# Attention and two mixture-of-experts stages on one core: counts in h's bank, later weight conversions, a shorter expert 3

## The chip, the cores and the metric

The kernel runs on one core of a Trainium2 chip. Its engines are PE (TensorE, with its weight loads shown as PEld), DVE (VectorE), ACT (ScalarE), POOL (GpSimd) and SP (SyncE); each runs its own list of instructions in order and meets the others by semaphores. The metric is the time of one execution on the device in microseconds (us), the median of several runs; lower is better.

## What is computed

Three steps follow one another. Attention over 4 batches of 8 heads has 576 positions, a head size of 64, a window of 128 positions and a bias that falls with distance. Its output, 2304 tokens of 512 numbers, goes through a dense layer, and that layer's result through eight experts of which each token takes one or none:

```python
h = x @ w_in                       # 512 -> 2048
g = s * np.maximum(h, 0.0)**2 + b
x = g @ w_out                      # 2048 -> 512
do_compute = x @ w_skip > 0        # the other tokens are passed on as they are
e_idx, gate_w = argmax and softmax of x @ w_gate over 8 experts
out[token] = x[token] + gate_w * (np.maximum(x[token] @ w1[e], 0) @ w2[e])
```

All of it is fp32. How many tokens each expert gets depends on the data: 639, 194, 63, 83, 51, 20, 167 and 143 for the inputs used here.

## The kernel before

**Products.** Each fp32 product is made of three products of a rounded type: an operand is split into a high part (names that end in h, made on ACT by a cast) and a low part (names that end in l, made on DVE by subtraction, helper `lower`, L77), and high by high, high by low and low by high are added up in PSUM.

**Dense layer.** The tokens are taken in six blocks (j = 0 to 5) of 384, and each block in 16 steps (m = 0 to 15, loop L704 to L752). One step is `g1(j, m)` (L457: 12 matmuls into the PSUM tile `h_ps`, then ACT's relu of it into `r`, L467, and DVE's square `r<-r,sb`, L468), `g1_split` (L471: `gh` on ACT, L477, and `gl` on DVE, L478) and `g2` of the step before (L483: nine matmuls into the three tiles `acc`). So PE runs 12 matmuls of h(m), nine of acc(m-1), 12 of h(m+1), and so on, in an order that the code writes out by hand (a chain from matmul to matmul, helper `mm`, L135). `h_ps` has one bank, "h", and `r` one buffer, so the relu of a step has to wait for `gl` of the step before. The bursts of the attention and its transposes (`t_ps`, in bank "at", copied to `pt` on ACT) and products (`o_ps`) stand between these steps where `events` (L331 to L352) puts them.

**Routing.** After a block, `logits` (DVE, three a step in the last block) and `route` (L532 to L640) work out for each token its expert and its place in that expert's list. In it two small matmuls count the tokens of each expert (L584 and L585, out of `oh` into `p_ps`, in bank "at"), DVE adds these counts to the running ones (`bs`, `v`, `cnt`, L601 to L603), and after more DVE work (`rk`, `di`) POOL writes the tokens' numbers into the lists in DRAM (`lst<-pay,di`, L637). For blocks 0 to 3 the counting stands in the next block but one, behind h of step 1; the counts of block 4 stand in the last block, behind step 10.

**Last block (j = 5).** While it runs, the weights of the first experts arrive in two ring buffers and are split, one piece after each step (`split`, L655: ACT's cast `wh<-ring`, L663, then DVE's `wl`, after which SP loads the next piece). The generator `moe2` is started there too (`later`): when the lists of blocks 0 to 4 are in DRAM, SP reads a part of them (`la<-lst`, L973), POOL gathers expert 0's first tokens by it (`two<-x2d,la`, L796), and PE transposes them (`x_t`, L799: `p_x<-cst,two`, L803) ahead of the last nine matmuls of acc.

**Experts.** `expert(e)` (L959) branches on the number of tiles of 128 tokens: `pair` (L925) for two or more, else `single` (L880). PE fetches its instructions as it goes, and `hint` (L858) tells it ahead of time where the branch of the next expert will lead. `FURTHER` (L33) says how many further pairs of tiles are written out in code for an expert ahead of a loop that takes the rest. `fin` (L841) makes an expert's result (`og`, DVE L843), `h_t` (L849) transposes the hidden layer (`p_t` on PE, `hth` on ACT, `htl` on DVE), and `conv` splits weight pieces for later experts.

## Time and profile before

| | us |
|---|---|
| median of three runs (743.21 to 746.54) | 743.6 |
| the profiled execution | 747.76 |
| its span, first to last instruction | 745.9 |
| PE busy in it | 719.0 (96%) |
| DVE busy | 522.3 (70%) |
| ACT busy | 373.1 (50%) |

The profile is of one execution, which took 4.2 us longer than the median. PE is busy nearly all the time, so what matters is where PE stands still, for whom, and in which stretches it was granted half its clock. Times in the rows are counted from the span's start. The attention and blocks 0 to 5 take up the time to about 545, the routing of the last block and expert 0 the time to about 604, and experts 1 to 7 the rest.

### The profile page before, as it was taken

The numbers are of one execution on the slowest core, as the hardware profiler recorded it, in microseconds if no ns is written. First come the engines' busy times: TensorE is split into PE (matmuls) and PEld (weight loads), VectorE is DVE, ScalarE is ACT, GpSimd is POOL, SyncE is SP. The second block draws the span as 40 slices with busy tenths as digits, with TensorE's granted clock in tenths as the row PEclk, the third lists the DMA queues.
The fourth block names the chain that finished last, engine by engine and source line by source line (L and its number), as shares of the span: only waits on it lengthen the run. The fifth ranks groups of instructions, "written<-read, shape, count | busy, mean of one in ns | idle before, by whom it ended". The sixth has DMA issues, their size and how long they took to land. (4 is left out here: it accounts for less than half of the span.)

```text
span 745.9 us, 13019 instructions
## 1 busy us (share of the span) xinstructions
PE 719.0 (96%) x4532; PEld 616.7 (83%) x4532; DVE 522.3 (70%) x1544; ACT 373.1 (50%) x889; POOL 61.3 (8%) x66
## 2 busy tenths in 40 slices
PE   6789999999999999999999999999999999899995
PEld 4468888888888888788888888988888888787994
DVE  4989999767677676777777665799753245799341
ACT  5766777544564444555555333445441134688230
POOL 0000000000001000100000100010205310312011
PEclk9779999999999999999999999999999999999999
DMA  8986441522324221432123111455442642989000
GB/s 244 294 279 177 132 142 40 168 68 81 93 61 125 54 68 54 138 92 80 54 79 110 31 42 43 156 173 180 128 170 81 226 137 79 359 293 383 19 21 17
DMA packets 50911, 96.40 MB, mean 129 GB/s; under 512 B 8874, under 2 KB 26282, under 8 KB 50816
## 3 DMA queue, kind: packets, MB, share of 16 engines
q1 hardware_dynamic: 45744, 86.35, 36.0%
q0 software_dynamic: 3296, 5.60, 2.3%
q10 hardware_dynamic: 1776, 3.28, 1.2%
q8 instruction: 49, 0.80, 0.4%
q14 instruction: 46, 0.38, 0.2%
HBM read 84.89 MB, written 13.65 MB: 132 GB/s over the span
## 5 line engine op out<-in xcount | busy, mean ns | idle before, releaser
L135 PE MATMUL h_ps<-xh,wh 128*128 128x384 f32 x380 | 132.4, 348 | 0.7 <-ACT r L467 0.7
L135 PE MATMUL h_ps<-xh,wl 128*128 128x384 f32 x380 | 128.9, 339 | 0.0
L135 PE MATMUL h_ps<-xl,wh 128*128 128x384 f32 x380 | 128.8, 339 | 0.0
L467 ACT ACTIVATE r<-h_ps 128x384 f32<-128x384 f32 x96 | 47.1, 490 | 135.5 <-PE h_ps L135 115.3
L468 DVE SCALAR_TENSOR_TENSOR r<-r,sb 128x384 f32<-128x384 f32 x96 | 59.1, 616 | 58.6 <-ACT r L467 57.6
L529 DVE CUSTOM_DVE_ANT_0 junk<-x,hp 128x512 bf16<-128x512 f32 x135 | 92.8, 688 | 1.6
L135 PE MATMUL acc<-wh,gh 128*128 128x512 f32 x288 | 86.4, 408 | 0.0
L177 ACT ACTIVATE tp<-tp,stat 128x256 f32<-128x256 f32 (+2 forms) x160 | 74.8, 469 | 19.4 <-DVE stat L169 19.3
L135 PE MATMUL acc<-wh,gl 128*128 128x512 f32 x288 | 83.0, 396 | 0.0
L135 PE MATMUL acc<-wl,gh 128*128 128x512 f32 x288 | 82.5, 394 | 0.0
L477 ACT ACTIVATE gh<-r,sb 128x384 fp32r<-128x384 f32 x96 | 59.1, 616 | 40.5 <-DVE r L468 40.3
L478 DVE SCALAR_TENSOR_TENSOR gl<-r,sb,gh 128x384 fp32r<-128x384 f32 x96 | 59.0, 615 | 28.2 <-ACT gh L477 28.0
L135 PEld LDWEIGHTS h_ps<-xh,wh 128*128 128x128 f32 x380 | 71.9, 189 | 6.9 <-issue 2.7
L135 PEld LDWEIGHTS h_ps<-xl,wh 128*128 128x128 f32 x380 | 72.0, 189 | 2.6
L135 PEld LDWEIGHTS h_ps<-xh,wl 128*128 128x128 f32 x380 | 71.9, 189 | 0.3 <-DVE wl L77 0.3
L135 PEld LDWEIGHTS acc<-wh,gl 128*128 128x128 f32 x288 | 53.9, 189 | 13.6 <-DVE gl L478 0.9
L135 PEld LDWEIGHTS acc<-wl,gh 128*128 128x128 f32 x288 | 54.1, 188 | 12.5
L169 DVE CUSTOM_DVE_ANT_0 tp<-s_ps,masks 128x256 f32<-128x256 f32 (+2 forms) x160 | 52.7, 377 | 10.5 <-PE t_ps L133 4.5
L637 POOL DMA_INDIRECT lst<-pay,di x18 | 18.5, 1030 | 490.9 <-DVE di L634 486.9
L135 PEld LDWEIGHTS acc<-wh,gh 128*128 128x128 f32 x288 | 50.0, 188 | 7.6 <-issue 3.1
L838 PE MATMUL p_o<-wh,hth 128*128 128x512 f32 x120 | 48.7, 405 | 0.3 <-ACT hth L854 0.2
L838 PE MATMUL p_o<-wl,hth 128*128 128x512 f32 x120 | 47.4, 395 | 0.0
(165 smaller groups left out, 1249.9 us busy)
## 6 DMA issues: line engine op xcount, KB each, us to landing
w_words<-wm SPq DMA_DIRECT2D x30, 512.0 KB
more<-we SPq DMA_DIRECT2D x30, 512.0 KB
ring<-we SPq DMA_DIRECT2D x28, 512.0 KB
hp<-wgt SPq DMA_DIRECT2D x45, 256.0 KB
vt<-vl SPq DMA_DIRECT2D x32, 192.0 KB
x2d<-x SPq DMA_DIRECT2D x17, 256.0 KB
out<-x SPq DMA_DIRECT2D x17, 256.0 KB
q<-q_in SPq DMA_DIRECT2D x16, 192.0 KB
```

Source lines behind the costliest of these rows:

```text
L135: i = f(*args, **kw)
L169: anchor['v'] = nc.vector.tensor_tensor_reduce(out=t[0:nr, i, c0:c0 + n], in0=ps[i][0:nr, c0:c0 + n], in1=masks[0:nr, 2 * units[u][1] + i, ...
L177: anchor['s'] = nc.scalar.activation(out=t[0:nr, i, c0:c0 + n], in_=t[0:nr, i, c0:c0 + n], func=ACTF.Exp, scale=-1.0, bias=st[0:nr, 0, i:i ...
L467: nc.scalar.activation(out=r, in_=hp, func=ACTF.Relu)
L468: nc.vector.scalar_tensor_tensor(out=r, in0=r, scalar=sb[:, 0:1], in1=r, op0=ALU.mult, op1=ALU.mult)
L477: nc.scalar.activation(out=gh, in_=r, func=ACTF.Identity, bias=sb[:, 1:2])
L478: i = nc.vector.scalar_tensor_tensor(out=gl, in0=r, scalar=sb[:, 1:2], in1=gh.bitcast(F32), op0=ALU.add, op1=ALU.subtract)
L529: nc.vector.tensor_tensor_reduce(out=junk, in0=x2t[j, t], in1=w, scale=1.0, scalar=0.0, op0=ALU.mult, op1=ALU.add, accum_out=lgs[j][:, t, ...
L637: i = nc.gpsimd.indirect_dma_start(out=lst, out_offset=bass.IndirectOffsetOnAxis(ap=di[:, t:t + 1], axis=0), in_=pay[:, t, :], in_offset=N ...
L838: last = nc.tensor.matmul(p_o[s], lhsT=h[:, c, s * 128:s * 128 + 128], rhs=w[p, 4 + c // 2][:, o:o + 512], start=cs[0] == 0 and n == 0, st ...
```

## The change

It has six parts. (1) The counts of blocks 0 to 3 go into columns 384 to 431 of the bank that holds `h_ps`, which is now taken whole (128 x 512), in place of bank "at". (2) In the last burst of the attention, the two transposing turns stand at 0.65 and 0.85 of the interval in place of 0.55 and 1. (3) In the last block, `h_ps` takes banks "h" and "as0" in turn, and the weight pieces are split behind `gh` on ACT and behind `gl` on DVE, at steps 1 to 13 and 15, with two more after the block's result; before, one was split at each of the 16 steps. (4) Expert 3 has no further pair written out, and the hint of expert 3's one-tile code stands two matmuls into the second half of its second product. (5) In `single`, the last piece of weights is split behind `fin` and `h_t`. (6) In `pair`, the second tile is transposed into a bank of `p_h`.

```diff
--- before.py
+++ after.py
@@ -30,7 +30,8 @@
 UB = 3
 CONV = (6, 7, 8, 9, 10, 11, 12)
 LAST = NE - 1
-FURTHER = (2, 0, 0, 1, 0, 0, 0, 0)
+LATE = 3
+FURTHER = (2, 0, 0, 0, 0, 0, 0, 0)
 
 
 
@@ -344,7 +345,7 @@
             d, at = first + i, 1 + wait + i * n_seg / n
             ev.append((at, burst, d))
             gs = groups[2 * d:2 * d + 2]
-            ts = [at + n_seg / n * f for f in ((0.55, 1) if j else (0.65, 0.85))]
+            ts = [at + n_seg / n * f for f in ((0.55, 1) if j and d + 1 < (len(groups) + 1) // 2 else (0.65, 0.85))]
             if ceil(ts[0]) == ceil(ts[1]):
                 ev.append((ts[1], turn2, gs))
             else:
@@ -455,8 +456,13 @@
     acc = {}
     UNTIL = [1, 2, 3, 4, 5, 5]
 
+    hs = {}
+
     def g1(j, m):
-        hp = bank("h", [128, TB], "h_ps")
+
+        hp = bank("as0" if j == NB - 1 and m % 2 else "h", [128, 512], "h_ps")
+        hs[j] = hp
+        hp = hp[:, 0:TB]
         n = 0
         for k in range(4):
             for w, x in ((wh[m], xh), (wh[m], xl), (wl[m], xh)):
@@ -474,11 +480,11 @@
         gh = M.tile([128, TB], F32R, name="gh", tag="gh", bufs=2)
         gl = M.tile([128, TB], F32R, name="gl", tag="gl", bufs=2)
 
-        nc.scalar.activation(out=gh, in_=r, func=ACTF.Identity, bias=sb[:, 1:2])
+        a = nc.scalar.activation(out=gh, in_=r, func=ACTF.Identity, bias=sb[:, 1:2])
         i = nc.vector.scalar_tensor_tensor(out=gl, in0=r, scalar=sb[:, 1:2], in1=gh.bitcast(F32),
                                            op0=ALU.add, op1=ALU.subtract)
         gt[j, m] = (gh, gl)
-        return i
+        return a, i
 
     def g2(j, m, ps=(0, 1, 2)):
         gh, gl = gt[j, m]
@@ -573,14 +579,14 @@
         off = rc[:, 8:16].unsqueeze(1).to_broadcast([128, TPB, NE])
         de = small([128, TPB], "de")
         eo = small([128, TPB], "eo", U32)
-        if j < NB - 1:
-            pp = bank("at", [128, 2, TPB, NE], "p_ps")
-        else:
-            pp = bank("as0", [128, 2, TPB, NE], "p_ps")
         f = nc.tensor.matmul
         if j < NB - 2:
             yield
+
+            pp = hs[j + 2][:, TB:TB + 2 * TPB * NE].rearrange("p (a t e) -> p a t e", a=2, t=TPB)
             f = lambda *args, **kw: mm(nc.tensor.matmul, *args, **kw)
+        else:
+            pp = bank("at" if j < NB - 1 else "as0", [128, 2, TPB, NE], "p_ps")
         f(pp[:, 0], lhsT=ustrict, rhs=oh.rearrange("p t e -> p (t e)"), start=True, stop=True)
         last = f(pp[:, 1], lhsT=ones, rhs=oh.rearrange("p t e -> p (t e)"), start=True, stop=True)
         nc.vector.tensor_tensor(out=v, in0=oh, in1=off, op=ALU.mult)
@@ -652,7 +658,7 @@
             eng.dma_start(out=ws.at[ws.loaded], in_=we[PIECES[ws.loaded]])
             ws.loaded += 1
 
-    def split():
+    def split(act=None, dve=None):
         n = ws.split
         t, i = PIECES[n]
         p = t % 2
@@ -660,8 +666,10 @@
             eh[p, i] = W(8 * p + i, "wh")
             el[p, i] = W(8 * p + i, "wl")
         raw = ws.at.pop(n)
-        nc.scalar.copy(eh[p, i], raw)
-        lower(el[p, i], raw, eh[p, i])
+        with tc.issue_after(act) if act else ExitStack():
+            nc.scalar.copy(eh[p, i], raw)
+        with tc.issue_after(dve) if dve else ExitStack():
+            lower(el[p, i], raw, eh[p, i])
         ws.free.append(raw)
         ws.split = n + 1
         pump()
@@ -719,7 +727,7 @@
                 next(counting, None)
                 counting = None
             attn_until(2 * m + 1)
-            done = g1_split(j, m)
+            biased, done = g1_split(j, m)
             if j == 0:
                 w_step()
             if m:
@@ -743,11 +751,16 @@
                     counting = route(j - 1)
                     next(counting, None)
             if j == NB - 1 and m in (10, 15):
-                later(None)
-            if j == NB - 1:
+                order[0] = later(None) or order[0]
+
+            if j == NB - 1 and 0 < m < NM - 2:
+                split(biased.ins, done.ins)
+            if j == NB - 1 and m == NM - 1:
                 split()
     last = g2(NB - 1, NM - 1)
     evac(NB - 1)
+    split()
+    split()
     spare = later(last.ins)
     for _ in route(NB - 1):
         pass
@@ -831,12 +844,14 @@
             nc.scalar.activation(out=h, in_=ps, func=ACTF.Relu)
             nc.vector.scalar_tensor_tensor(out=l, in0=ps, scalar=0.0, in1=h.bitcast(F32), op0=ALU.max, op1=ALU.subtract)
 
-    def gemm2(p, s, f, cs=None):
+    def gemm2(p, s, f, cs=None, then=None):
         cs = cs or range(4 * f, 4 * f + 4)
         for n, (c, h, w) in enumerate([(c, hth, w) for c in cs for w in (eh, el)] + [(c, htl, eh) for c in cs]):
             o = (c % 2) * 512
             last = nc.tensor.matmul(p_o[s], lhsT=h[:, c, s * 128:s * 128 + 128], rhs=w[p, 4 + c // 2][:, o:o + 512],
                                     start=cs[0] == 0 and n == 0, stop=cs[-1] == 7 and n == 3 * len(cs) - 1)
+            if n == 1 and then:
+                hint(*then)
         return last
 
     def fin(s, x, e, k):
@@ -888,16 +903,18 @@
         gemm1(e % 2, 0)
         conv(own)
         gemm1(e % 2, 1)
-        hint(e + 1, 1)
+        if e != LATE:
+            hint(e + 1, 1)
         conv(new, 2)
         gemm2((e - 1) % 2, 1, 0)
         if e < LAST:
             x_t(one[(e + 1) % 4], 0)
-        conv(new)
-        gemm2((e - 1) % 2, 1, 1)
+        conv(new, 1)
+        gemm2((e - 1) % 2, 1, 1, then=(e + 1, 1) if e == LATE else None)
         fin(1, *rest(e - 1))
         h_t()
         nc.vector.tensor_copy(la[:, e, 1, :], la[:, e, 0, :])
+        conv(new)
         if e == LAST:
             second(e)
             fin(1, one[e % 4], e, 1)
@@ -926,7 +943,7 @@
 
         left = rest(e if e == 0 else e - 1)
         own = [p for p in NEED[e] if p[0] == e] if e else []
-        x_t(rows1[0], 1)
+        x_t(rows1[0], 1, p_h[1])
         conv(own, 2)
         second(e - (e > 0))
         fin(1, *left)
@@ -974,9 +991,9 @@
     gather(0, 0, two[1], NT - TB)
     yield
     p_x = bank("at", "p_x")
-    x_t(two[1], 0)
-
-    with tc.issue_after((yield)):
+    last = x_t(two[1], 0)
+
+    with tc.issue_after((yield last.ins)):
         p_h = [bank("ao", "p_h0"), bank("as1", "p_h1")]
         gemm1(0, 0, (0, 1))
     with tc.issue_after((yield og)):
```

What stands where, from the two programs, with the semaphores that an instruction waits for in brackets. PE in block 3, behind h of step 1 (`oh` and `cst` are the operands of the counts), before:

```order
L135 MATMUL h_ps<-xl,wh_354 128x384
L135 MATMUL h_ps<-xh,wl_355 128x384
L135 MATMUL p_ps<-oh,cst 128x24 [waits DVE_49,PE_49]
L135 MATMUL p_ps<-oh,cst 128x24
L135 MATMUL t_ps<-cst,tp 128x128 [waits DVE_49,PE_49]
L135 MATMUL t_ps<-cst,tp 128x128 x3
L135 MATMUL acc<-wh_273,gh 128x512 [waits Activation_49]
```

and now:

```order
L136 MATMUL h_ps<-xl,wh_354 128x384
L136 MATMUL h_ps<-xh,wl_355 128x384
L136 MATMUL h_ps<-oh,cst 128x24 [waits Activation_49]
L136 MATMUL h_ps<-oh,cst 128x24
L136 MATMUL t_ps<-cst,tp 128x128 [waits DVE_49,PE_49]
L136 MATMUL t_ps<-cst,tp 128x128
L136 MATMUL t_ps<-cst,tp 128x128 [waits DVE_49]
L136 MATMUL t_ps<-cst,tp 128x128
L136 MATMUL acc<-wh_273,gh 128x512
L136 MATMUL acc<-wh_273,gh 128x512 [waits DVE_49]
```

The counts waited for DVE and PE, and wait for ACT now; `t_ps`, which waited for DVE's use of the counts, waits for its own operand.

DVE in the last block, behind the square of step 12 and the sums of block 4's counts (the rows named `r<-r,sb` are the squares of step 13 and later; the last two instructions `di<-rk,di` and `di<-di,eo` make the places that POOL's list writing waits for), before:

```order
L629 TENSOR_REDUCE rk<-v 128x3 [waits DVE_49]
L599 COPY bs<-cnt 128x8 [waits DVE_49]
L632 TENSOR_SCALAR di<-rk 128x3 [waits DVE_49]
L633 SCALAR_TENSOR_TENSOR di<-rk,di 128x3 [waits DVE_49]
L634 TENSOR_TENSOR di<-di,eo 128x3 [waits DVE_49]
L77 TENSOR_TENSOR wl_6086<-ring_5484,wh_6085 128x1024 [waits DMAHW4_49,Activation_49]
L478 SCALAR_TENSOR_TENSOR gl<-r,sb,gh 128x384 [waits Activation_49]
L468 SCALAR_TENSOR_TENSOR r<-r,sb 128x384 [waits Activation_49]
L77 TENSOR_TENSOR wl_6120<-ring_5483,wh_6119 128x1024 [waits DMAHW5_49,Activation_49]
L478 SCALAR_TENSOR_TENSOR gl<-r,sb,gh 128x384 [waits Activation_49]
```

and now:

```order
L635 TENSOR_REDUCE rk<-v 128x3 [waits DVE_49]
L605 COPY bs<-cnt 128x8 [waits DVE_49]
L638 TENSOR_SCALAR di<-rk 128x3 [waits DVE_49]
L78 TENSOR_TENSOR wl_6111<-ring_5480,wh_6110 128x1024 [waits DMAHW4_49,Activation_49]
L639 SCALAR_TENSOR_TENSOR di<-rk,di 128x3 [waits DVE_49]
L474 SCALAR_TENSOR_TENSOR r<-r,sb 128x384 [waits Activation_49]
L640 TENSOR_TENSOR di<-di,eo 128x3 [waits DVE_49]
L484 SCALAR_TENSOR_TENSOR gl<-r,sb,gh 128x384 [waits PE_49,Activation_49]
L78 TENSOR_TENSOR wl_6145<-ring_5479,wh_6144 128x1024 [waits DMAHW5_49,Activation_49]
L474 SCALAR_TENSOR_TENSOR r<-r,sb 128x384 [waits Activation_49]
L484 SCALAR_TENSOR_TENSOR gl<-r,sb,gh 128x384 [waits PE_49,Activation_49]
L474 SCALAR_TENSOR_TENSOR r<-r,sb 128x384 [waits Activation_49]
```

The last `di` stood ahead of the conversion `wl` and of the next step's `r`; it stands behind both. `gl` stands ahead of the step's `wl` and no longer behind it.

DVE at the end of expert 5, before:

```order
L806 TENSOR_TENSOR xtl<-p_x,xth 128x4x128 [waits Activation_49]
L77 TENSOR_TENSOR wl_6052<-more_6480,wh_6051 128x1024 [waits DMAHW0_49,Activation_49]
L77 TENSOR_TENSOR wl_6086<-more_6481,wh_6085 128x1024 [waits DMAHW1_49,Activation_49]
L843 SCALAR_TENSOR_TENSOR og<-p_o_6360,la,one_6033 128x512 [waits DMASW3_49,DMASW5_49,DMASW2_49,DMASW6_49,DVE_49,PE_49]
L855 TENSOR_TENSOR htl<-p_t_6358,hth 128x4x128 [waits Activation_49]
L855 TENSOR_TENSOR htl<-p_t_6359,hth 128x4x128 [waits Activation_49]
L900 COPY la<-la 128x2 [waits DMASW0_49]
L964 UNCONDITIONAL_BRANCH
```

and now:

```order
L819 TENSOR_TENSOR xtl<-p_x,xth 128x4x128 [waits Activation_49]
L78 TENSOR_TENSOR wl_6077<-more_6476,wh_6076 128x1024 [waits DMAHW0_49,Activation_49]
L858 SCALAR_TENSOR_TENSOR og<-p_o_6356,la,one_6024 128x512 [waits DMASW3_49,DMASW5_49,DMASW2_49,DMASW6_49,DVE_49,PE_49]
L870 TENSOR_TENSOR htl<-p_t_6354,hth 128x4x128 [waits Activation_49]
L870 TENSOR_TENSOR htl<-p_t_6355,hth 128x4x128 [waits Activation_49]
L916 COPY la<-la 128x2 [waits DMASW0_49]
L78 TENSOR_TENSOR wl_6111<-more_6477,wh_6110 128x1024 [waits DMAHW1_49,Activation_49]
L981 UNCONDITIONAL_BRANCH
```

One of the two `wl` has moved behind `og`, both `htl` and the copy of `la`.

## Rows read from the trace of the kernel before

**Rows 1.** The page's part 1: engine, busy us (share of the span), instructions.

```profile
PE 719.0 (96%) x4532; PEld 616.7 (83%) x4532; DVE 522.3 (70%) x1544; ACT 373.1 (50%) x889; POOL 61.3 (8%) x66
```

**Rows 2.** PE's waits: operation, whom for; us in total, times, longest.

```profile
PE p_h L813 <- ACT wh L663: 2.1, 1, 2.1
```

**Rows 3.** Timeline at block 2's counts: start, us, instruction [idle before <-releaser].

```profile
226.17 0.52 PE L135 MATMUL p_ps<-oh,cst 128*128 128x24 f32 x4
...
226.54 0.94 PE L135 MATMUL acc<-wh,gh 128*128 128x512 f32 x3
```

**Rows 4.** Timeline at block 3's counts.

```profile
309.57 0.52 PE L135 MATMUL p_ps<-oh,cst 128*128 128x24 f32 x4
309.77 0.49 ACT L467 ACTIVATE r<-h_ps 128x384 f32<-128x384 f32 x1 [1.20 <-PE h_ps L135]
...
311.22 0.17 DVE L602 COPY cnt<-bs 128x8 f32<-128x8 f32 x1
...
311.42 0.63 PE L135 MATMUL t_ps<-cst,tp 128*128 128x128 f32 x4 [1.32 <-DVE cnt L602]
```

**Rows 5.** Timeline of PE at the attention's last burst.

```profile
455.78 1.04 PE L135 MATMUL o_ps<-pt,vt 64*64 64x64 f32 x16 [0.51 <-ACT pt L217]
```

**Rows 6.** Timeline of steps 12 to 15 of the last block: PE, ACT and DVE.

```profile
531.19 0.85 PE L135 MATMUL acc<-wh,gh 128*128 128x512 f32 x3
...
536.95 0.45 PE L135 MATMUL h_ps<-xh,wh 128*128 128x384 f32 x1 [0.73 <-ACT r L467]
...
536.41 0.49 ACT L467 ACTIVATE r<-h_ps 128x384 f32<-128x384 f32 x1 [1.37 <-DVE gl L478]
...
534.56 1.23 DVE L77 TENSOR_TENSOR wl<-ring,wh 128x1024 fp32r<-128x1024 f32 x1 [1.22 <-ACT wh L663]
535.70 0.61 DVE L478 SCALAR_TENSOR_TENSOR gl<-r,sb,gh 128x384 fp32r<-128x384 f32 x1
```

**Rows 7.** Timeline of block 4's lists and the two gathers: DVE, POOL, SP, PE.

```profile
529.70 0.16 DVE L634 TENSOR_TENSOR di<-di,eo 128x3 uint32<-128x3 uint32 x1
...
530.14 0.97 POOL L637 DMA_INDIRECT lst<-pay,di  x1 [40.24 <-DVE di L634]
...
537.85 1.04 POOL L796 DMA_INDIRECT two<-x2d,la  x1 [4.16 <-DMA la<-lst]
...
562.26 1.00 POOL L796 DMA_INDIRECT one<-x2d,la  x1 [0.30 <-issue]
...
535.53 0.33 SPq L973 DMA_DIRECT2D la<-lst  x1
...
542.63 0.60 PE L803 MATMUL p_x<-cst,two 128*128 128x128 f32 x4
...
566.00 0.63 PE L803 MATMUL p_o<-cst,one 128*128 128x128 f32 x4 [0.93 <-DMA one<-x2d,la]
```

**Rows 8.** Windows: us from:to, length, engines' busy us, PE clock, DMA share, GB/s.

```profile
311.40:314.80 3.40, 3.38 (x25) 2.62 (x27) 2.41 (x11) 0.99 (x4) 0.68 (x1) 1.00 0.76 238
...
644.40:647.70 3.30, 1.25 (x6) 1.05 (x6) 3.30 (x6) 2.63 (x4) 1.33 (x2) 1.00 1.01 403
647.75:651.15 3.40, 3.40 (x10) 2.62 (x9) 1.21 (x2) 0.20 (x1) 1.97 (x2) 0.50 1.03 386
```

**Rows 9.** Timeline from expert 5 to expert 6: PE, DVE, ACT.

```profile
684.74 1.04 PE L851 MATMUL p_t<-cst,r 128*128 128x128 f32 x8
686.18 0.66 PE L803 MATMUL p_x<-cst,two 128*128 128x128 f32 x4 [0.40 <-DVE wl L77]
686.93 0.48 PE L838 MATMUL p_o<-wh,hth 128*128 128x512 f32 x1
...
683.76 2.36 DVE L77 TENSOR_TENSOR wl<-more,wh 128x1024 fp32r<-128x1024 f32 x2 [0.26 <-ACT wh L663]
686.04 0.74 DVE L843 SCALAR_TENSOR_TENSOR og<-p_o,la,one 128x512 f32<-128x512 f32 x1
...
685.42 1.07 ACT L854 CAST hth<-p_t 128x512 fp32r<-128x512 f32 x2 [0.74 <-ACT wh L663]
```

**Rows 10.** PE's branches at L964, into each expert's code: duration ns min/median/max.

```profile
L964 PEldq COMPARE_BRANCH  x7: 82/343/5128, 604.6 to 706.7; - x7
```

## The prediction

> **What bounds the kernel now.** The page's busy times come first: PE works in 96% of the span [rows 1], so the other engines matter only where PE stands still for them, and every us that PE waits is a us of the result. The list of PE's waits says where that is; its largest late entry is 2.1 us at the start of expert 3 [rows 2]. The timelines then show who ends each wait. Block 3's counts hold up `t_ps` for 1.32 us, since both use bank "at" and DVE's `cnt` reads it last [rows 4]. The attention's last `o_ps` waits 0.51 us for `pt` [rows 5]. In the last block h of step 15 waits 0.73 us for the relu of step 14, which waited for `gl` of step 13, which stood behind a weight conversion `wl` of 1.23 us [rows 6]. At expert 6 `p_x` waits 0.40 us for `wl`, and the next product starts only when `og` and `hth` are there [rows 9]. The change goes at all four. What I looked for next is what each repair makes late, by following in the two programs what each moved instruction waits for now.
>
> **The counts, blocks 0 to 3.** What goes is the wait of `t_ps`: in block 2, with no wait, the next instruction starts 0.37 us after the counts [rows 3], so in block 3 `t_ps` could have started at 309.94 in place of 311.42 [rows 4]: 1.48 us less, once. What comes is a new wait. The counts lie in the bank that the relu of the same step is reading, and in the new order the first of them waits for ACT, for exactly this relu. PE had gone straight on: the counts start at 309.57 and the relu runs from 309.77 to 310.26 [rows 4]. With about 0.03 us from the end of an instruction to PE's start (`cnt` ends at 311.39, `t_ps` starts at 311.42 [rows 4]) they start at 310.29, 0.72 us later. ACT is idle ahead of that relu, so it cannot come earlier, and nothing stands on PE beside it, since acc and the next h are queued behind the counts. There are four such counts, one each for blocks 0 to 3: 4 x 0.72 = 2.9 us. DVE's sums come 0.7 us later too, but the next h, which has to wait for them, stands behind nine acc matmuls. This part gives 2.9 - 1.48 = +1.4 us.
>
> In the trace of before the counts run during the relu, in another bank [rows 3, 4]. [...]
>
> **The attention's last turns.** `t_ps` now stands ahead of nine acc matmuls, which take about 2 us, and `pt` is copied under them. The wait of 0.51 us [rows 5] goes: -0.5.
>
> **The last block.** With two banks h(15) need not wait, -0.8 us (the idle 0.73 and a slow restart [rows 6]). `gl` now comes ahead of `wl`, and so earlier, at each step. The 16 conversions remain, and their loads start one step later; the last of them belong to expert 1, whose weights are wanted 50 us later, so these cost nothing.
>
> But `di`, the last step on DVE of block 4's lists, is pushed back. Before, it ended at 529.86 [rows 7]. Now it stands behind a `wl` and behind the square of step 13, and that square needs step 13's relu. h(13) ends on PE where acc starts, at 531.19 [rows 6]; the relu starts 0.2 us behind its h and takes 0.49 [rows 4], to 531.88; the square takes 0.62 and `di` 0.16, so `di` ends at about 532.6, 2.75 us later than before. All behind it moves by that: POOL's list writing (first at 530.14), SP's `la` (535.53) and the gather of `two` (537.85) [rows 7], which goes to about 540.6. How long the gather takes to reach PE shows at the other gather, where PE did wait: issue at 562.26, PE on at 566.00, 3.74 us [rows 7]. So before, `two` was ready at 541.6 and `p_x` at 542.63 didn't wait; now it is ready at 544.35, while PE gets there at 541.8. PE waits about 2.5 us, acc of step 15 and all that follows are queued behind it, and PE is busy afterwards, so nothing gives it back. Against before, `p_x` starts 1.7 us later; I take 1.6, since that other gather shared its queue with one just ahead. The part costs +1.6 in all, where without the late `di` it would give -0.8.
>
> **The clock.** [...] Half the clock for 3.4 us costs up to 1.6 us. [...]
>
> **Experts.** At expert 6, `p_x` goes to a bank of `p_h` and no longer waits for a conversion's use of its old one, and `og` (686.04) stands behind one `wl` less (each 1.2 us [rows 9]), so it ends near 685.7. What is late next is the first of the two `hth`, which ends at 686.0; the product starts near 686.1 in place of 686.93: -0.8. At the other pairs no wait is marked and I count nothing; it could be some tenths. In the singles the last conversion comes later, for an expert two further on: nothing.
>
> **Code.** Expert 3's unused pair and the moved hint change only where code lies and when it is fetched. One of PE's seven branches took 5.128 us, the median 0.343 [rows 10]; the long one is that into expert 3, behind which PE stood 2.05 us [rows 2]. Ahead of that branch PE's code is two instructions shorter and otherwise the same, so I expect it to last: 0, with bounds of -3.6 (the wait of 2.05 and the 1.6 of its half clock go) and +3.6 (another branch becomes such).
>
> **Sum.** 1.4 - 0.5 + 1.6 + 0.8 - 0.8 = +2.5 us. The profiled execution took 747.76, so its like would take 750.3; against the median of 743.6 that is 746.1. I put the change on the median, since nothing in it hangs on what made the profiled execution longer.
>
> **Rivals.**
> 1. The gather is not missed: `di` or the data come earlier than I work out, or the reading of `la` had slack. For it speaks that before there was 1 us in hand; against it, that the order on DVE is fixed and the relu of step 13 can't be early. Then the last block gives -0.8 and there is no idle time for the clock: 1.4 - 0.5 - 0.8 - 0.8 = -0.7, 742.9.
> 2. The branch into expert 3 finds its code, since its target moves with the shorter code: -3.6 on the forecast, 742.5. For it: six of seven branches do [rows 10]. Against: the hint and the branch that missed are where they were.
> 3. Slower: the branch into expert 4 misses. The hint in expert 3 is given about 22 matmuls of the last product and transposes before that branch instead of a half expert ahead. If the fetch takes longer than PE's queued work lasts, PE stands still as at expert 3, 2.05 us, with the half clock behind it: +3.6, 749.7. It decides from the point where hint and queued work together are shorter than the fetch; the branch into expert 3 shows that over 5 us can be needed at worst [rows 10]. [...]
>
> **Chances.** Forecast 0.52, rival 1 0.17, rival 2 0.12, rival 3 0.14, others 0.05. The range takes in rivals 1 and 2 at their times less the tenths not counted and rival 3: 742.0 to 749.7. About 0.5%, 3.7 us, is what a measurement here can tell from no change: 739.9 to 747.3. Slower by more is rival 3 and a forecast with the whole clock term and a longer wait: 0.23. Faster by more needs rivals 1 and 2 at once or a gain that I don't see: 0.09. That leaves 0.68.
>
> **What would show it.** PE's waits of after should hold four of about 0.7 us at the counts for the relu, none of `t_ps` for `cnt`, and one of 2 to 3 us of `p_x` for the gather of `two`, with h(15) not waiting. DVE's last `di` of block 4 should end behind the square of step 13. `p_o` of expert 6 should start 0.4 to 0.5 us after its `p_x`. If PE goes through the counts without idling, or the gather is there in time, the forecast is wrong by the terms above. The row of branches decides between forecast and rivals 2 and 3.

## The result, and the profile after

The changed kernel takes 753.0 us (median of six runs, 752.1 to 755.8) against 743.9 us before (six runs, 743.1 to 746.5): 1.0122 times the time, 95% interval 1.0100 to 1.0145, so 9.2 us slower. The forecast was 746.1 us, range 742.0 to 749.7, most likely no difference that can be measured. It was wrong, and the time lies outside the range. The profiled execution took 753.98 us with a span of 752.1 us; that of before took 747.76 us, 3.9 us over its median, so these two traces show only part of the difference. The last experiment took a second trace of each.

PE works 721.1 us, 2.1 us more than in [rows 1]; the rest of the difference is idle time. This is the list of PE's waits of after (operation, whom for; us in total, times, longest):

```profile
PE p_x L816 <- DMA two<-x2d,la: 5.0, 1, 5.0
...
PE h_ps L136 <- ACT r L473: 2.3, 4, 0.6
PE p_h L826 <- ACT wh L670: 2.0, 1, 2.0
...
PE p_h L826 <- issue: 0.6, 2, 0.3
```

The four counts wait for the relu, as forecast; no `t_ps` waits for `cnt` any more, and h of step 15 doesn't wait. The wait of `p_x` for the gather of `two` is there, but it is 5.0 us and not 2.5. The wait into expert 3 is what it was [rows 2]. Two waits of 0.3 us ahead of `p_h` are new.

The counts of block 3, timeline of after:

```profile
309.19 0.34 PE L136 MATMUL h_ps<-xh,wl 128*128 128x384 f32 x1
309.56 0.49 ACT L473 ACTIVATE r<-h_ps 128x384 f32<-128x384 f32 x1 [1.20 <-PE h_ps L136]
310.11 0.62 PE L136 MATMUL h_ps<-oh,cst 128*128 128x24 f32 x4 [0.58 <-ACT r L473]
310.58 0.63 PE L136 MATMUL t_ps<-cst,tp 128*128 128x128 f32 x4
```

In [rows 4] the relu ran beside the counts; here they start 0.06 us behind its end.

Then the lists of block 4 and the first gather, timeline of after (DVE, POOL, SP's queue, PE):

```profile
530.48 1.23 DVE L78 TENSOR_TENSOR wl<-ring,wh 128x1024 fp32r<-128x1024 f32 x1
531.62 0.15 DVE L639 SCALAR_TENSOR_TENSOR di<-rk,di 128x3 uint32<-128x3 uint32 x1
...
532.04 0.62 DVE L474 SCALAR_TENSOR_TENSOR r<-r,sb 128x384 f32<-128x384 f32 x1 [0.26 <-ACT r L473]
532.58 0.15 DVE L640 TENSOR_TENSOR di<-di,eo 128x3 uint32<-128x3 uint32 x1
...
533.01 0.97 POOL L643 DMA_INDIRECT lst<-pay,di  x1 [42.65 <-DVE di L640]
...
535.56 1.21 POOL L643 DMA_INDIRECT lst<-pay,di  x1 [0.30 <-issue]
535.94 0.33 SPq L658 DMA_DIRECT2D ring<-we  x1
539.78 0.33 SPq L990 DMA_DIRECT2D la<-lst  x1
542.28 1.18 POOL L809 DMA_INDIRECT two<-x2d,la  x1 [5.52 <-issue]
542.58 0.33 SPq L658 DMA_DIRECT2D ring<-we  x1
...
546.93 1.09 PE L816 MATMUL p_x<-cst,two 128*128 128x128 f32 x4 [4.96 <-DMA two<-x2d,la]
```

`di` ends at 532.73 (forecast: about 532.6) and the first list write comes 2.87 us later than in [rows 7]. But `la`, the reading of the lists, comes 4.25 us later, and `p_x` follows the gather's issue by 4.65 us, where 3.74 was expected. A load of the ring (`ring<-we`, 512 KB) is issued at 535.94, ahead of the end of the last list write, and another at 542.58, 0.30 us behind the gather. In the kernel before, that first load stood behind `la`, and no load was issued beside the gather (SP's queue and the last list write, before):

```profile
532.72 0.97 POOL L637 DMA_INDIRECT lst<-pay,di  x1 [0.30 <-issue]
...
535.95 0.38 SPq L652 DMA_DIRECT2D ring<-we  x1
```

Behind the wait PE was granted about half its clock, 0.55 (window of after; columns as in [rows 8]):

```profile
546.93:551.30 4.37, 4.37 (x14) 3.60 (x14) 0.72 (x2) 0.85 (x2) 0.00 (x0) 0.55 0.22 90
```

The same stretch, from `p_x` to the first `p_h`, had taken 2.53 us in the trace of before.

Lining up the PE starts of two traces, instruction by instruction, gives where the time comes from. "First pair" is the two traces above; "second pair" the last two experiments, one more execution of each kernel. The row of `p_x` is how much later it starts, the row below it what the stretch from there to the first `p_h` lasts longer (4.37 and 4.14 us against 2.53). All in us, each entry rounded by itself:

| place | forecast | first pair | second pair |
|---|---|---|---|
| first 60 us | 0 | -1.1 | -1.0 |
| counts, four places | +1.4 | +1.9 | +1.9 |
| attention's last turns | -0.5 | -0.4 | -0.4 |
| two acc starts early in the last block | 0 | -0.3 | -0.3 |
| h of step 15 | -0.8 | -1.0 | -1.0 |
| `p_x` for the gather | +2.4 | +5.1 | +5.1 |
| half clock right behind it | +0.8 | +1.8 | +1.6 |
| clock in the last routing | 0 | +1.6 | -1.6 |
| experts 1 and 2 | 0 | -0.1 | -0.1 |
| into expert 3 and the clock behind it | 0 | -1.6 | +1.3 |
| into expert 4 | 0 | +0.5 | +4.0 |
| into expert 5 | 0 | +0.5 | +0.5 |
| expert 6 | -0.8 | -0.9 | -0.9 |
| sum | +2.5 | +6.1 | +9.2 |

### The profile page after: what moved, and what is told of

The parts are those of the page before. It is cut to its first block, busy times and chain, and to the rows that moved or that the text cites. A ratio compares the mean times of both kernels' runs of the same rounds, so it can differ in the third digit from the quotient of the medians.

```text
span 752.1 us, 13022 instructions
## 1 busy us (share of the span) xinstructions
PE 721.1 (96%) x4532; PEld 618.4 (82%) x4532; DVE 523.0 (70%) x1544; ACT 373.9 (50%) x889; POOL 65.4 (9%) x66
```

## The experiments

After the result two theories stood for the gather. **Late order:** the 5 us are all from DVE's order, `di` behind `wl` and the square, as the prediction had it, only mis-sized. **Loads:** about 2 us are from that; the rest is from the ring loads that come ahead of and beside the small transfers. Further theories concern experts 3 to 5.

### The parts one by one

**The change without its last block** (part 3 undone). Edit, in its main lines:

```diff
-        hp = bank("as0" if j == NB - 1 and m % 2 else "h", [128, 512], "h_ps")
+        hp = bank("h", [128, 512], "h_ps")
...
-            if j == NB - 1 and 0 < m < NM - 2:
-                split(biased.ins, done.ins)
-            if j == NB - 1 and m == NM - 1:
+            if j == NB - 1:
                 split()
```

Without the two conversions behind the block, too.

> The changed kernel with its part 3 undone: one bank for h in the last block, one conversion at every step and ahead of gl, as before. Theory A (the last block is the cause: the gather of two comes too late, and the idle PE loses its clock): of the 7.7 us that the trace of after shows there, all go; what is left is about +2.0 for the counts, -0.4 for the attention's turns and about 0 for the experts, so 745 to 746 us, and no wait of p_x for two. Theory B (the runs of before mostly don't have the fetch wait at expert 3 that its profiled execution had, and the changed code has it always): 3.5 us more, 748.5 to 749.5.

Measured: 747.3 us against 744.8, ratio 1.0039 (1.0018 to 1.0060). `p_x` doesn't wait. So part 3 makes most of the loss, some 6 to 7 us, and the other parts together also cost. The wait into expert 3 is longer than in any other trace:

```profile
PE p_h L818 <- ACT wh L668: 3.7, 1, 3.7
PE p_h L818 <- issue: 0.6, 2, 0.3
```

**The counts alone** (the kernel before with part 1).

> The kernel before with part 1 alone: the counts of blocks 0 to 3 in columns 384 to 431 of h's bank. Theory (the relu of the same step is waited for): four PE waits of about 0.6 us, 0.85 us each from start to start, less the 1.48 us wait of t_ps: +1.9 us, about 745.8. Rival (columns of a bank are independent): -1.5 us, about 742.4.

Measured: 745.4 us against 744.8, ratio 1.0011 (0.9992 to 1.0030). The trace gives +0.9, -0.6, +0.8 and +0.8 at the four places, +1.9, of which the time can show no more than a part. PE's `h_ps` waits for the relu five times (3.1 us), the counts and h of step 15.

**The last block alone** (the kernel before with part 3).

> The kernel before with part 3 alone: two banks for h in the last block, conversions behind gh and gl. Theory A: h(15) doesn't wait (-0.9), p_x waits 5 us for two, half the clock behind it: +6.5 to +7.7, so 750 to 751.5. Rival: the late gather needs the shift that the counts bring, and alone it costs no more than the 2.5 us that I had predicted: 745 to 746.

Measured: 750.8 us against 744.8, ratio 1.0093 (1.0062 to 1.0124). Timeline of POOL, SP and PE:

```profile
533.23 1.20 POOL L637 DMA_INDIRECT lst<-pay,di  x1 [0.30 <-issue]
533.61 0.33 SPq L652 DMA_DIRECT2D ring<-we  x1
537.36 0.33 SPq L980 DMA_DIRECT2D la<-lst  x1
539.72 1.42 POOL L803 DMA_INDIRECT two<-x2d,la  x1 [5.29 <-issue]
...
544.54 1.09 PE L810 MATMUL p_x<-cst,two 128*128 128x128 f32 x4 [4.91 <-DMA two<-x2d,la]
```

The same pattern without any other part: the load is issued 0.8 us ahead of the end of the last list write, `la` 2.93 us behind that end, `p_x` 4.82 us behind the gather. The counts and the experts have no hand in it.

**The experts' parts alone** (the kernel before with parts 4, 5 and 6).

> The kernel before with parts 4, 5 and 6 alone: no further pair in expert 3 and its later hint, the last conversion behind h_t in the one-tile code, the second tile in a bank of p_h. Theory A: -0.3 at expert 1, -0.9 at expert 6, +0.5 each at the starts of experts 4 and 5: about -0.1, 743.7. Theory B (the shorter code makes the fetch wait at expert 3 appear in every run): about +3.4, 747.

Measured: 745.5 us against 744.8, ratio 1.0015 (0.9984 to 1.0046), from 741.1 to 750.7, a wider scatter than any other kernel here. The trace shows -0.9 at expert 6 as forecast, and +0.5 into each of experts 4 and 5, which the prediction did not have.

### The wait for the gather

**Loads held back.** The changed kernel, but the loads that follow the conversions of steps 13 and 15 are issued behind `la`; DVE's order stays.

```diff
-                split(biased.ins, done.ins)
+                split(biased.ins, done.ins, load=m < NM - 3)
             if j == NB - 1 and m == NM - 1:
-                split()
+                split(load=False)
...
     evac(NB - 1)
+    with tc.issue_after(ns.la_dma.ins):
+        pump()
...
```

> The changed kernel; of the weight loads, those that follow the conversions of steps 13 and 15 of the last block are issued behind the read of block 4's list (la) and no longer ahead of it. DVE's order is that of the changed kernel. Theory C (half of the 5.0 us that p_x waits is DVE's late di, as predicted, and half is that the list writes and the read of la share the DMA rings with a 512 KB weight load): la is issued about 5.7 us behind di, at about 538.3, and p_x waits about 2.5 us. Rival (the list chain is long by itself): la stays near 539.8 and p_x waits 5 us.

Measured: one time, 748.8 us against 744.1. Timeline:

```profile
531.53 0.15 DVE L640 TENSOR_TENSOR di<-di,eo 128x3 uint32<-128x3 uint32 x1
...
534.52 1.20 POOL L643 DMA_INDIRECT lst<-pay,di  x1 [0.30 <-issue]
536.90 0.33 SPq L994 DMA_DIRECT2D la<-lst  x1
537.32 0.39 SPq L658 DMA_DIRECT2D ring<-we  x1
539.27 1.04 POOL L813 DMA_INDIRECT two<-x2d,la  x1 [3.55 <-DMA la<-lst]
...
542.86 1.06 PE L820 MATMUL p_x<-cst,two 128*128 128x128 f32 x4 [1.93 <-DMA two<-x2d,la]
```

The wait falls from 4.96 to 1.93 us with nothing changed but the loads' place. `la` now comes 1.18 us behind the end of the last list write in place of 3.01 (1.83 us less), and `p_x` 3.59 us behind the gather in place of 4.65 (1.06 less); with 0.13 from `la` to the gather that is the whole 3.0 us. The late order on DVE is worth the rest, 1.9 us. In the kernel before `la` stood 1.84 us behind the last list write, 0.66 more than here; with that the late order alone would make some 2.6 us, which is the 2.5 of the prediction. The loads' theory holds in the times; what the two transfers share is not shown.

The records of the single DMA packets in the two traces show the same. In the changed kernel the last list write's packets ran from 538.46 to 539.18, 2.90 us behind its issue, and those of the ring load from 536.92 to 539.17. With the load held back the list write's ran from 536.32 to 536.48, 1.80 us behind its issue, with no packet of a load at that time. The gather's began 2.98 us behind its issue in the changed kernel, with a load running, and 1.76 us behind it here.

**Places first.** The changed kernel, but the last `di` is put ahead of step 12's conversion and of step 13's square on DVE.

```diff
...
+        with tc.issue_after(places[0]) if j == NB - 1 and m == 13 else ExitStack():
             nc.vector.scalar_tensor_tensor(out=r, in0=r, scalar=sb[:, 0:1], in1=r, op0=ALU.mult, op1=ALU.mult)
...
-                split(biased.ins, done.ins)
+                split(biased.ins, places[0] if m == 12 else done.ins)
```

> The changed kernel with two instructions of DVE's order changed: the last di of block 4 stands ahead of the conversion of step 12 and ahead of the square of step 13. Loads are as in the changed kernel. Theory C: di ends about 2 us earlier, near 530.8, the list is read behind the load that is still ahead of it on SP, and p_x waits 1 to 2 us in place of 5.0; 3.5 to 5 us faster than the changed kernel in its trace. Rival: the wait is set by the loads alone and stays at 4 to 5 us.

Measured: one time, 750.2 us against 744.1. `p_x` waits 0.47 us. Since that order also put the second load behind `la`, both causes are gone here and the run doesn't part them; what it shows is that with both gone the wait nearly is:

```profile
535.50 0.97 POOL L647 DMA_INDIRECT lst<-pay,di  x1 [0.30 <-issue]
537.65 0.33 SPq L994 DMA_DIRECT2D la<-lst  x1
538.07 0.39 SPq L662 DMA_DIRECT2D ring<-we  x1
539.98 1.05 POOL L813 DMA_INDIRECT two<-x2d,la  x1 [3.50 <-DMA la<-lst]
...
543.62 0.63 PE L820 MATMUL p_x<-cst,two 128*128 128x128 f32 x4 [0.47 <-DMA two<-x2d,la]
```

Again `la` comes 1.18 us behind the list write, and `p_x` 3.64 us behind the gather. That the time is still 6 us over before has other causes, and the largest is the third rival's: in this execution the branch into expert 4 took 5.7 us, and the start of expert 4 moved by 4.4 us against the second trace of before (0.5 of it is the next section's). PE's waits, and that branch alone:

```profile
PE p_h L830 <- ACT wh L674: 5.4, 2, 2.7
```

```profile
L985 PEldq COMPARE_BRANCH  x1: 5718/5718/5718, 656.0 to 656.0; - x1
```

### Experts 4 and 5

PE's first product of an expert waits for a place in ACT's list of the expert before. Counted from that list's end it is the third instruction in both programs; before, that was a cast `wh` long done, and with the last conversion behind `h_t` it is the first `hth`:

```profile
666.37 1.07 ACT L869 CAST hth<-p_t 128x512 fp32r<-128x512 f32 x2 [1.65 <-PE p_t L866]
...
667.05 0.47 PE L826 MATMUL p_h<-wh,xth 128*128 128x512 f32 x1 [0.28 <-issue]
```

The two casts take 1.07 us, so the first ends at 666.95, 0.1 us ahead of `p_h`; at the next expert it ends at 679.98, and `p_h` starts at 680.08. The rival was that the changed code of part 4 makes it. The next kernel leaves part 5 out and keeps 4 and 6.

> The kernel before with parts 4 and 6 alone, so as the run of the experts' parts but with every conversion of the one-tile code in its old place. Theory D (the first product of the next expert waits for a place in ACT's list, counted over both branches; at that place stood a long finished conversion, and since part 5 a transposed copy hth stands there): the 0.5 us at the starts of experts 4 and 5 vanish, while p_x at experts 1 and 6 keeps -0.3 and a part of -0.9. Rival (the later hint or the shorter code makes them): they stay.

Measured: one time, 745.0 us against 744.1. The +0.5 into experts 4 and 5 are gone, with part 4 still in. So part 5 makes them, by the wait above. The gain of 0.9 at expert 6 is gone too, with the bank of part 6 still in: it needs `og` ahead of the last conversion (part 5). Whether it needs that bank as well was not tried; no kernel had part 5 without part 6.

### What is worth keeping

**Two banks alone.** The kernel before, where h of the last block takes banks "h" and "as0" in turn and nothing else.

> The kernel before with one thing of part 3 alone: h of the last block takes banks h and as0 in turn, while the conversions stay where they were. Theory A (the second bank is good, the moved conversions are what costs): h(15) starts 0.9 us earlier, p_x doesn't wait for two or by 0.1 us only: -0.9 us. Rival (an earlier PE alone runs into the gather of two): the gain is lost at p_x, 0.

Measured: 742.2 us against 744.5, ratio 0.9978 (0.9959 to 0.9998). h of step 15 gives -1.0 and `p_x` doesn't wait; the rest of the 2.2 us is not placed. The conversions' order did the harm, not the banks.

**Counts behind three acc matmuls.** The kernel before with the counts in h's bank, but behind the first three acc matmuls in place of ahead of all nine, so that the relu is over when they come:

```diff
...
+                if counting and m == 1:
+                    g2(j, 0, (0,))
+                    next(counting, None)
+                    counting = None
+                    g2(j, 0, (1, 2))
...
```

> The kernel before with part 1 alone and the counts behind the first three acc matmuls of the step, 0.7 us later on PE than in the change. Theory (the cost of the spare columns is the relu of the same bank, and nothing else): no PE wait for the relu, up to 0.2 us at each of the four places for the sums ahead of the next h, and the 1.48 us wait of t_ps gone: -0.7 to -1.5 us. Rival (sharing the bank costs by itself): +1 or more, as with the counts right behind h.

Measured: 742.7 us against 744.5, ratio 0.9973 (0.9960 to 0.9987). At the four places the trace shows -1.5 for block 3 and +0.15 to +0.17 for each of the others, -1.0 in all; the rest of the 1.8 us is not placed. The wait of `t_ps` is gone without the four waits for the relu.

**The parts that pay, together.** Both of these, the attention's turns (part 2), the bank of `p_h` for the second tile (part 6), and the last conversion behind `h_t` in expert 5 only, the one in front of the pair of expert 6. Conversions of the last block, code and hints are those of before. Its expectation was written before the two kernels above had run.

> The kernel before with what the traces show to gain and without what they show to cost: the counts in h's bank, but behind the first three acc matmuls, so that the relu is over when they start; the attention's turns; two banks for h in the last block with the conversions where they were; the second tile in a bank of p_h; the last conversion behind h_t in expert 5 alone. Terms from the traces: -1.5 (t_ps no longer waits for cnt, and the relu isn't waited for), -0.4, -0.9, -0.3 and -0.9: -4.0 us, about 740.8 where before is 744.8. Rival: the counts still cost a wait, of h of step 2 for DVE's sums, up to 0.5 us at each of four places, and the gather of two is just missed: -1 to -2.

Measured: 739.0 us against 744.1, ratio 0.9928 (0.9905 to 0.9952). It beats both kernels. The lists and the gather:

```profile
529.48 0.97 POOL L641 DMA_INDIRECT lst<-pay,di  x1 [0.30 <-issue]
532.45 0.33 SPq L981 DMA_DIRECT2D la<-lst  x1
...
534.77 1.04 POOL L803 DMA_INDIRECT two<-x2d,la  x1 [4.32 <-DMA la<-lst]
538.41 0.60 PE L810 MATMUL p_x<-cst,two 128*128 128x128 f32 x4
```

`p_x` has no idle time ahead of it. Of the waits in [rows 2, 4 to 6, 9] only the one into expert 3 is left, 2.1 us. Against the second trace of before the places named give -1.0 (counts), -0.4, -1.0, -0.3 (expert 1) and -0.8, together -3.5 of the 5.1 us; the rest lies in the first 60 us, in the clock of the last routing and at expert 3, which differ between executions of one kernel.

### A second trace of each

The first pair of traces left 3 of the 9.2 us open, and its largest terms besides the gather were clock stretches. So both kernels ran once more.

> The kernel before, unchanged, for a second trace of it. The places from block 2's counts on explain 7.2 us between the two traces so far, the medians differ by 9.2. Theory A: the rest is in half-clock stretches and a slow start-up that only the first trace of before had (552.2 to 555.6 us, behind expert 3's wait, and 1 us before 54 us); this trace then reaches its first counts 1 us earlier or more, has one half-clock stretch less, about 1.4 us, and takes 743 to 745.5. Rival: the stretches belong to the kernel; this trace shows both again at the same places and takes about 747. In both, t_ps waits 1.3 us for cnt, h of step 15 0.7 us for the relu, and p_x doesn't wait for the gather.

> The changed kernel, unchanged, for a second trace of it. Theory: what belongs to the kernel comes again: p_x waits 4.9 to 5.0 us for the gather of two with half the clock behind it, la is issued 3.0 us behind the start of the last list write's end (536.8 to 539.8), three counts cost 0.8 each, and experts 4 and 5 start 0.5 us later each. Rival: the wait for the gather depends on where packets fall and is under 4 us this time. The wait into expert 3 and the half-clock stretches of the routing, which differed from trace to trace, may differ again: 1.0 to 3.7 us, and one stretch or two. Time 752 to 754.

Measured: 744.1 us (before) and 753.3 us (after), each near its median. Waits of the changed kernel:

```profile
PE p_x L816 <- DMA two<-x2d,la: 4.9, 1, 4.9
PE p_h L826 <- ACT wh L670: 4.6, 2, 2.4
...
PE h_ps L136 <- ACT r L473: 2.3, 4, 0.6
```

Its list chain again has the load 0.8 us ahead of the end of the list write, `la` 2.89 us behind it and `p_x` 4.77 us behind the gather; the rival that the wait depends on chance falls. The table's second column shows what came again and what didn't. The first trace of before had a wait of 2.05 us into expert 3 and a granted clock of 0.50 behind it for 3.4 us; the second has 1.1 us, and 1.00 for the 3.4 us behind it:

```profile
PE p_h L813 <- DVE og L843: 1.1, 1, 1.1
```

The half-clock stretch of the last routing, on the other hand, is there again in before (the -1.6 of the table's second column), so half of that expectation fell. New in the second trace of after is a long branch into expert 4, called a miss here: it took 5.24 us, where the first trace of after had 0.45:

```profile
L981 PEldq COMPARE_BRANCH  x1: 5242/5242/5242, 659.5 to 659.5; - x1
```

```profile
L981 PEldq COMPARE_BRANCH  x1: 447/447/447, 663.5 to 663.5; - x1
```

PE waited 2.17 us for it and ran at a granted clock of 0.57 behind that (first window; the second, at 1.00, is that behind the wait of 2.43 us into expert 3):

```profile
664.89:668.29 3.40, 3.40 (x9) 2.72 (x10) 2.98 (x3) 1.35 (x2) 3.10 (x2) 0.57 0.78 226
649.98:653.38 3.40, 3.40 (x15) 2.77 (x16) 2.71 (x3) 1.37 (x3) 3.10 (x2) 1.00 0.83 281
```

Of the +4.0 into expert 4, 0.5 are part 5's, so the miss cost 3.4 us. It shows in two of the seven traces of kernels with part 4 and in none of the seven without it. The branch into expert 4 tells more than PE's wait: with part 4 it took 0.45 us twice, 1.5 to 1.8 us three times (PE waited 0.3 us or less there) and over 5 us twice; without part 4 it took 0.35 to 0.45 us all seven times. The wait into expert 3 is longer with part 4 as well, 1.7 to 3.7 us (mean 2.5) against 1.0 to 2.1 (mean 1.5). That fits the later hint of expert 3, its shorter code and the wide scatter of the experts' parts alone, but no kernel had part 4 by itself, and each trace is one execution: that part 4 makes both is likely and not shown.

## Why the prediction was wrong

**The counts: right in mechanism, a third short.** Four waits for the relu came, and the wait of `t_ps` went, by -1.48 net of the new cost. Each costs 0.85 us and not 0.72: the counts start 0.75 us later against the h ahead of them, and take 0.10 us longer to the next instruction (0.47 against 0.37 in [rows 3]). Together +1.9 against +1.4. The order makes the counts wait for the relu of the same bank; that this wait is needed was the author's assumption, and no run went without it.

**The attention's turns, h of step 15, expert 6: right.** -0.4, -1.0 and -0.9 against -0.5, -0.8 and -0.8. That the earlier `gl` brings two acc starts of the last block forward by 0.3 us was not counted.

**The last block: the step that failed.** The prediction followed `di` rightly behind `wl` and the square, and its end to 0.15 us. Then it let "all behind it" move "by that", and of the loads it said that they "start one step later" and "cost nothing", because it priced them only by when their weights are wanted. It did not ask what else they pass. SP issues a load when the conversion ahead of it frees a buffer, here 0.03 us behind the conversion's end (535.91 and 535.94), and the two pushes met: `la` now waited for list writes that came 2.87 us later, and the load that had followed `la` by 0.42 us now ran 3.8 us ahead of it, over the last list write's packets. That cost 1.2 us there against before, and the next load 1.0 us at the gather. The other gather of [rows 7] gave 3.74 us, and 3.6 was right for a gather without a load beside it; but this one had one. `p_x` moved by +5.1 in place of +2.4. These 2.7 us, with the 0.9 that the half clock behind the wait cost more than the forecast had (below), are 3.6 of the 6.7 us between the forecast's +2.5 and the measured +9.2.

In the trace of after the packets of POOL's list write and gather go through one queue (q0), those of SP's loads through another (q1). Even so, with SP's load under way the way from the last list write's end to `la` took 1.83 us longer and that from the gather to `p_x` 1.06 us longer than with the loads held back. Beside the row in [rows 7] stands the question which the prediction left out: what runs together with the list write and the gather.

**The clock: it fell as feared, at twice the price, and the forecast was blind elsewhere.** No run shows the 0.8 of the sum: it was the author's middle between two outcomes, 0 and 1.6, which the windows of 1.00 and 0.50 in [rows 8] gave, behind waits of 1.32 and 2.05 us. Behind the gather's wait PE's granted clock was 0.50 and 0.51 for 3.4 us in the two traces of after, and the stretch to the first `p_h` lasted 1.8 and 1.6 us longer, so the measured cost is the upper outcome or a little over it. And the stretches of the last routing (granted clock 0.50 for 3.4 us from 552.2 in the first trace of before, for 6.8 us from 557.7 in that of after) and behind expert 3 moved the time by -1.6 to +1.6 us between executions of the same two kernels. The forecast treated the ones of before as fixed.

**The singles: "nothing" was wrong, twice 0.5 us.** The prediction asked only when the converted weights are wanted. It did not ask who waits on ACT's list by position: PE's first product of the next expert did.

**Code: the forecast's zero and rival 3.** Rival 2 fell: in all 14 traces PE waits at the branch into expert 3, from 1.0 to 3.7 us. Its premise, that six of seven branches find their code, read too much into [rows 10]: the branch into expert 2 took 3.1 us in the first trace of before (628.41 to 631.52), and PE didn't wait only because its queued products lasted to 631.67. The forecast's zero for expert 3 is doubtful too, by the longer waits with part 4. Rival 1 fell with the gather. Rival 3's mechanism, a miss into expert 4 at +3.6, came in one of the two traces of after, at 3.4. It was set up as all or nothing, and is neither.

**The sum.** To the forecast's +2.5 come 2.7 for the gather, 0.9 for the half clock behind it, 1.0 for experts 4 and 5 and 0.5 for the counts, all in both pairs, less 0.3 for the acc starts and 0.2 for h of step 15: +7.1. The 2.1 us left to 9.2 lie in what differs from one execution to the next, the miss into expert 4, the wait into expert 3 and the half-clock stretches; two pairs are too few to divide them. The 1.0 to 1.1 us by which after is ahead in the first 60 us of both pairs, where q and k are loaded, need not be the change: the second trace of before is itself 1.1 us ahead of the first there, and the 14 traces lie between 0.2 us behind it and 2.9 ahead.

## What to carry to other kernels

When an instruction that frees a buffer is moved, write down the transfer that its buffer triggers, and lay it over every small transfer on the critical path, list writes and gathers above all: 512 KB beside them cost more here (3.0 us) than the late instruction did (1.9 us). When work is put at the end of an engine's list, look who waits on that list by position across a branch. And a wait for a bank's reader cost little here with other matmuls between the reader and the writer: the same counts, moved behind three matmuls, cost 0.15 to 0.17 us a place in place of 0.85, and the part became a gain.

## What the runs showed of the hardware

**Small transfers beside a large load.** The reading `la` was issued 1.18 us behind the end of the last list write where the load before it was issued 3.4 or 5.0 us ahead of that end (two traces), 1.84 to 2.07 us where a load was issued 2.1 us ahead of that end (nine traces, the two of before among them), and 2.89 to 3.01 us where a load was issued 0.8 us ahead of it (three traces). The first gather reached PE 3.59 and 3.64 us behind its issue without a load beside it, and 4.65 to 4.82 us with one (three traces).

**The clock behind idle time.** Of the waits into experts 3 and 4 and for the first gather in all 14 traces, the six from 0.47 to 1.70 us were followed by 3.4 us at a granted clock of 1.00. Of the fifteen from 1.93 to 4.96 us, eleven were followed by 3.4 us at a mean granted clock of 0.50 to 0.70, and four by 1.00, behind 1.99, 2.09, 2.43 and 2.73 us. This is the one of 2.09 us, in the fastest kernel:

```profile
640.14:643.54 3.40, 3.40 (x15) 2.77 (x16) 2.45 (x4) 0.80 (x2) 2.43 (x3) 1.00 1.04 402
```

**The same branch, short and long.** The changed kernel's branch into expert 4 took 0.45 us in one execution and 5.24 us in the other. The first traces of before and after also have packets of instructions all through the span (q8, 49 packets of 16 KB, 0.80 MB): one of them ran within each branch into an expert that took over 3 us, as from 643.92 to 644.80 in the 5.13 us branch of before, and none within those under 0.5 us. Whether the branch waited for that packet is not shown.
